# Attention and soft mixture of experts on one core: another written order, copies on the other engine, masks as steps of their own

## The chip, the core and the metric

The kernel runs on one core of one Trainium2 chip. The core has five instruction streams that run side by side and wait for each other by semaphores: TensorE (PE in the profile), VectorE (DVE), ScalarE (ACT), GpSimd (POOL) and SyncE (SP), which here only issues DMA transfers. Each stream runs in its own program order, so an instruction that waits holds back everything behind it in its stream. The metric is the time of one execution on the device, in microseconds (us).

## The reference

Attention over q, k and v of shape 8 x 8 heads x 576 x 64, with a mask by blocks of 64 (a block sees itself and earlier ones), then a soft mixture of 8 experts with 4 slots each on the result.

```python
scores = scale * np.matmul(q, k.transpose(0, 1, 3, 2))
mask = block_i >= block_j                      # blocks of 64 positions
attn = softmax(np.where(mask, scores, -1e9))
x = (attn @ v), heads side by side             # 4608 x 512
logits = x @ phi                               # 4608 x 32 slots
d = softmax of logits over tokens;  slot_input = d.T @ x
slot_out[e] = np.maximum(slot_input[e] @ w1[e], 0.0) @ w2[e]
c = softmax of logits over slots;   out = c @ slot_out
```

All of it is computed in float32.

## The kernel before, in words

The attention works through 32 pairs of heads, four pairs to one of the 8 batch entries. Pair m goes through these steps; the short names are the keys of the table `TM`:

- `lq`, `lk`, `lv` (SP, L403 to L418): DMA loads of q, k (288 KB each) and v (256 KB and a tail of 32 KB). q and k have two buffers and v has two, so the load for pair m+2 waits until PE is through with pair m.
- `ks` (POOL, L424): scales k in place. It waits for the landing of k.
- `UA`, `UB`, `UC` (PE, L464 and L485): the score tiles. The two 512 wide ones (`7`) come from UA, those of 576, 256, 192, 128 and 64 columns (`8`, `3`, `2`, `1`, `0`) from UB, and the two of 384 columns (`5`) from UC.
- `rm` (DVE, L507): row maximum of each tile. Ahead of the first `rm7` and of `rm5` the same function fills the masked 64 x 64 corners with a large negative number (L502, L505).
- `ex` (ACT, L517): exponential with the sum of each row. `ze` (POOL, L527) and `z` (DVE, L523): the inverses of the sums. `nm` (POOL, L534): the tile times its inverse, in place.
- `g7`, `gc`, `gd`, `g5` (PE, L554): transposes of the tiles by 64 x 64 blocks. gc takes tile 8, gd takes 3, 2, 1 and 0. `eg` and `og` (ACT L390 or DVE L392) copy them from PSUM to SBUF.
- `pv0`, `pv1`, `pa` (PE, L592 and L602): probabilities times v. `xb`, `xa`: copies of the result.

Between these stand the steps of the mixture for each batch entry: logits (`prt`), running maxima (`stats`), transposes of x (`xq`, `xn4`), and the weighted sums over tokens (`sl`, `sl4`). The weights of the experts come as 32 pieces of 1 MB each (L311): 18 go to places that nothing else uses, spread over the attention, and the others to places that the attention gives free. After pair 31 (from about 306 us on) the experts and the output follow.

The order is written out by hand: `TM` gives each step a time, steps are sorted by it, and each engine executes its steps in that order. The numbers of TM set nothing but the order. `EN` says for each copy whether ACT or DVE makes it, `BK` in which PSUM bank a step writes. Pairs 0 to 3 and the last two have their own entries (suffixes A to D, w and y); the others share four sets by m modulo 4 (suffixes .0 to .3). At L845 to L860 the steps get their times; L908 to L934 worked out from the times of the last readers when a weight piece may go to a place of the attention.

Of the kernel before, what the change touches and what calls it, by code (L numbers as in the profile page):

```python
# [21 lines left out]
NQ = 5  # L22
# [23 lines left out]
for name, n in (  # L46
# [18 lines left out]
    "T": 9.2, "lkA": -5.94771, "lqA": -2.81305, "lkB": -10.95031, "lqB": -8.91013, "ksA": -4.780053, "UAA":  # L65
# [3 lines left out]
    "ksB": -9.311415, "ze0A": 0.484236, "z0A": 4.153612, "ksC": 6.81181, "lkD": 5.110368, "rm8A": 4.053924, "lvA":  # L69
# [161 lines left out]
def tile_attention_softmoe(  # L231
# [99 lines left out]
    with ExitStack() as c1:  # L331
# [64 lines left out]
        def at(t, fn, *args):  # L396
            ops.append((t, len(ops), fn, args))
# [93 lines left out]
        def rowmax(m, x):  # L491
# [7 lines left out]
            if EN.get("Q" + x[0]) == "h":  # L499
                if x == "5":  # L500
                    for _, n, sc in todo:
                        nc.vector.memset(sc[0:64, :, 320:384] if n == 2 else sc[0:64, 320:384], NEG)  # L502
# [662 lines left out]
```

## Time and profile before

| what | us |
|---|---|
| median of 3 runs | 358.9 |
| the runs | 357.26, 358.90, 358.92 |
| span of the profiled execution | 357.1 |
| PE busy in that span | 342.2 (96%) |
| ACT, DVE, POOL busy | 272.0, 261.5, 205.0 |

The time of the profiled execution itself is not among the three runs. A run's time holds its span and a little around it; the lowest of the runs is 0.2 us above the span. PE's granted clock is full in all slices but the last. In the profile, an engine's idle time is given with what ended it; ends of matmuls are modelled, so that a short wait of PE can be hidden in a busy stretch.

### The profile page before, as it was taken

How to read it: one execution, taken by the hardware profiler on the slowest of the kernel's cores; microseconds unless marked ns; L12 is line 12 of the kernel's file. 1: busy time of each engine (PE TensorE's matmuls, PEld its weight loads, DVE VectorE, ACT ScalarE, POOL GpSimd, SP SyncE). 2: the span in 40 equal slices, each digit the busy share in tenths (PEclk: the TensorE clock that was granted, in tenths of full speed). 3: DMA queues.
4: the chain of work that ended last, by engine and by line, in shares of the span. 5: the costliest groups of instructions: out<-in, count | busy, mean ns of one | idle time of the engine just before them, and what ended most of it. 6: DMA issues, size and time to landing. Idle time of an engine off the chain costs nothing.

```text
span 357.1 us, 14425 instructions
## 1 busy us (share of the span) xinstructions
PE 342.2 (96%) x5724; PEld 237.1 (66%) x5724; DVE 261.5 (73%) x748; ACT 272.0 (76%) x869; POOL 205.0 (57%) x471
## 2 busy tenths in 40 slices
PE   8999999999999999999999999999999999999991
PEld 3767776677666766776767676776677677436750
DVE  4977777868887888777877887788888777462552
ACT  3988989888988898889888988899888875121441
POOL 3886767666766676567656766676687582000000
PEclk9999999999999999999999999999999999999996
DMA  6566526563664365743843556428333189999897
GB/s 198 182 211 229 163 74 212 199 225 101 184 224 133 102 218 186 249 106 114 292 135 101 204 195 211 148 70 312 127 104 102 36 253 331 375 397 397 327 373 298
DMA packets 29938, 72.29 MB, mean 202 GB/s; under 512 B 6960, under 2 KB 15280, under 8 KB 25520
## 3 DMA queue, kind: packets, MB, share of 16 engines
q1 hardware_dynamic: 29872, 71.38, 57.8%
q8 instruction: 45, 0.74, 0.8%
q14 instruction: 21, 0.17, 0.1%
HBM read 61.93 MB, written 9.44 MB: 200 GB/s over the span
## 4 chain that ended last, share of the span: by engine, by line
PE 79%; DVE 10%; POOL 5%; issue 3%; ACT 1%; DVEq 0%; POOLq 0%
PE one L592 15%; PE one L554 14%; PE one L464 7%; PE duo L464 7%; PE one L602 6%; PE one L485 5%; DVE stat L507 5%; POOL arena L534 4%; PE one L1088 4%; PE one L326 4%; PE duo L485 3%; PE one L1041 2%; PE one L623 2%; PE one L792 2%; DVE arena L392 1%
## 5 line engine op out<-in xcount | busy, mean ns | idle before, releaser
L534 POOL TENSOR_SCALAR arena<-arena,stat 128x512 f32<-128x512 f32 (+6 forms) x288 | 152.2, 544 | 30.8 <-DVE one L505 13.2
L517 ACT ACTIVATE arena<-one,stat 128x512 f32<-128x512 f32 (+5 forms) x194 | 93.9, 501 | 8.4 <-DVE stat L507 7.0
L390 ACT COPY arena<-one 128x384 f32<-128x384 f32 (+2 forms) x170 | 79.2, 503 | 26.8 <-PE one L554 21.3
L554 PEld LDWEIGHTS one<-ident,arena 64*128 64x128 f32 x1600 | 65.6, 138 | 33.4 <-ACT arena L390 9.0
L554 PE MATMUL one<-ident,arena 64*128 64x64 f32 x1600 | 76.3, 228 | 3.5 <-DVE arena L392 2.1
L507 DVE TENSOR_REDUCE stat<-one 128x1 f32<-128x512 f32 (+5 forms) x194 | 78.3, 436 | 1.7 <-PE one L485 0.6
L592 PE MATMUL one<-arena 128*64 128x256 f32 (+2 forms) x640 | 76.1, 384 | 0.0
L392 DVE COPY arena<-one 128x384 f32<-128x384 f32 (+3 forms) x106 | 56.4, 541 | 23.6 <-PE one L592 17.6
L517 ACT ACTIVATE arena<-duo,stat 128x384 f32<-128x384 f32 (+1 forms) x94 | 59.6, 640 | 7.0 <-DVE stat L523 5.6
L507 DVE TENSOR_REDUCE stat<-duo 128x1 f32<-128x576 f32 (+1 forms) x63 | 53.9, 855 | 13.3 <-PE duo L485 7.9
L592 PEld LDWEIGHTS one<-arena 128*64 128x64 f32 x640 | 41.1, 137 | 29.8 <-issue 18.2
L527 POOL TENSOR_SCALAR stat<-stat 128x2 f32<-128x2 f32 (+1 forms) x96 | 18.7, 195 | 55.0 <-ACT arena L517 50.9
L485 PE MATMUL one<-arena 64*64 64x256 f32 (+3 forms) x512 | 42.0, 303 | 0.0
L517 ACT ACTIVATION_READ_ACCUMULATOR arena<-one,stat 128x1 f32 x194 | 41.3, 213 | 0.0
L485 PE MATMUL duo<-arena 64*64 64x288 f32 x256 | 38.3, 417 | 0.0
L464 PE MATMUL one<-arena 64*128 64x512 f32 (+1 forms) x132 | 38.1, 636 | 0.0
L485 PEld LDWEIGHTS one<-arena 64*64 64x64 f32 x512 | 35.7, 133 | 2.2 <-ACT arena L517 0.4
L464 PE MATMUL duo<-arena 64*128 64x384 f32 x124 | 28.0, 529 | 0.4 <-ACT arena L517 0.4
L602 PE MATMUL one<-arena 128*64 128x64 f32 x620 | 24.9, 227 | 0.4 <-ACT arena L390 0.4
L602 PEld LDWEIGHTS one<-arena 128*64 128x64 f32 x620 | 20.6, 137 | 5.9 <-ACT xn L390 2.7
L424 POOL TENSOR_SCALAR arena<-arena 128x576 f32<-128x576 f32 x32 | 21.5, 672 | 3.6 <-DMA arena<-in_k 3.0
L523 DVE RECIPROCAL stat<-stat 128x2 f32<-128x2 f32 (+1 forms) x96 | 15.8, 165 | 7.2 <-POOL stat L527 6.9
(157 smaller groups left out, 382.8 us busy)
## 6 DMA issues: line engine op xcount, KB each, us to landing
arena<-in_w SPq DMA_DIRECT2D x31, 1024.0 KB, 7.2
arena<-in_k SPq DMA_DIRECT2D x32, 288.0 KB, 3.1
arena<-in_q SPq DMA_DIRECT2D x32, 288.0 KB, 3.2
arena<-in_v SPq DMA_DIRECT2D x32, 256.0 KB, 3.5
out<-arena SPq DMA_DIRECT2D x12, 512.0 KB, 4.5
out<-arena SPq DMA_DIRECT2D x2, 1024.0 KB, 5.6
arena<-in_v SPq DMA_DIRECT2D x32, 32.0 KB, 3.4
xarea<-in_w SPq DMA_DIRECT2D x1, 1024.0 KB, 8.0
```

Of the source, the lines that this page charges most:

```text
L390: nc.scalar.copy(out=out, in_=in_)
L392: nc.vector.tensor_copy(out=out, in_=in_)
L424: nc.gpsimd.tensor_scalar(out=area(f"ks{m % NQB}"), in0=area(f"ks{m % NQB}"), scalar1=SCALE, scalar2=0.0, op0=ALU.mult, op1=ALU.add)
L464: nc.tensor.matmul(scores(t + str(j), m)[o, a:e], lhsT=q[r, lo + o.start:lo + o.stop], rhs=k[r, a:e], start=True, stop=True)
L485: nc.tensor.matmul(o, lhsT=a, rhs=b, start=True, stop=True)
L507: nc.vector.tensor_reduce(out=st[:, 0, u:u + n], in_=sc, axis=AX.XY if x == "8" else AX.X, op=ALU.max, negate=True)
L517: nc.scalar.activation(out=pr, in_=sc, func=AF.Exp, bias=st[:, 0, u:u + 1], accum_out=st[:, 1, u:u + 1],)
L527: nc.gpsimd.tensor_scalar(out=st[:, 2, c], in0=st[:, 1, c], scalar1=EPS, scalar2=1.0, op0=ALU.add, op1=ALU.mult)
L534: nc.gpsimd.tensor_scalar(out=pr, in0=pr, scalar1=st[:, 2, u:u + 1], scalar2=0.0, op0=ALU.mult, op1=ALU.add)
L554: nc.tensor.transpose(out=trbank(m, g)[i][:, 64 * n:64 * n + 64], in_=prob(m, x)[r, 128 * c:128 * c + 128], identity=ident[r, r],)
L592: nc.tensor.matmul(xps[m, 0][64 * j:64 * j + 64, lo:hi], lhsT=vs(m)[:, j, c, :], rhs=rhs, start=a, stop=z, skip_group_check=True,)
L602: nc.tensor.matmul(xps[m, 1][64 * j:64 * j + 64, 0:64], lhsT=vs(m)[:, j, c, :], rhs=arena[:, lo:lo + 64], start=(c == 0), stop=(c == NQ - 1),)
```

## The change

The table TM is new: nearly every step has another number, and the order of the engines follows from it. `EN` puts 12 copies of the four steady sets and of the mixture on the other engine, six each way, and a number of those of the first and the last pairs. `BK` gives some steps another PSUM bank. The fill of the masked corners is no longer a part of `rowmax`: it is a step `mask` with two times of its own per pair (`mk7`, `mk5`). The weight pieces that go to places of the attention have times of their own (`pc0` to `pc6`) in place of computed ones. The diff cut to its code, with one line of the tables:

```diff
 TM = {
-    "T": 9.2, "lkA": -5.94771, "lqA": -2.81305, "lkB": -10.95031, "lqB": -8.91013, "ksA": -4.780053, "UAA":
+    "T": 9.2, "lkA": -63.498943, "lqA": -54.803813, "lkB": -52.245575, "lqB": -51.593279, "ksA": -50.318905, "UAA":
...
@@ rowmax
-            if EN.get("Q" + x[0]) == "h":
-                if x == "5":
-                    for _, n, sc in todo:
-                        nc.vector.memset(sc[0:64, :, 320:384] if n == 2 else sc[0:64, 320:384], NEG)
-                elif (tm(m, "rm" + x), x) == min((tm(m, f"rm7{j}"), f"7{j}") for j in range(2)):
-                    for j in range(2):
-                        nc.vector.memset(scores(f"7{j}", m)[0:64, 448:512], NEG)
             for u, n, sc in todo:
                 nc.vector.tensor_reduce(
...
+        def mask(m, x):
+            i, n = bank("S" + x, sfx(m)), NC[x]
+            if i in WIDE:
+                nc.vector.memset(duo[i].rearrange("p (j c) -> p j c", j=2)[0:64, :, n - 64:n], NEG)
+            else:
+                for t in two(i):
+                    nc.vector.memset(t[0:64, n - 64:n], NEG)
...
+            for x in "75":
+                at(t0 + tm(m, f"mk{x}"), mask, m, x)
...
-        places = []
-        for o in range(0, W0, PIECE):
-            places.append((max(ends[k] for k, (lo, hi) in AREAS.items() if lo < o + PIECE and hi > o), o))
...
-        for t, dst in places:
-            at(t, load_piece, nxt, dst)
-            nxt += 1
+        places = [arena[:, o:o + PIECE] for o in range(0, W0, PIECE)] + [xarea[:, 0:PIECE]]
+        for i, dst in enumerate(places):
+            at(tb + TM[f"pc{i}z"], load_piece, RES + i, dst)
+        nxt = RES + len(places)
```

Three places of the order follow. Line numbers of the changed kernel are higher by 5 or 6 here: L534 and L540 are `nm`, L527 and L533 `ze`, L424 and L429 `ks`, L407 and L412 `lk`, L414 and L419 with L418 and L423 `lv`, L311 and L316 the weight pieces.

**Place 1, the first pairs.** On POOL before, at the end of pair 1 (stat_119 belongs to odd pairs, stat_118 to even ones):

```order
L534 TENSOR_SCALAR arena<-arena,stat_119 128x128
L527 TENSOR_SCALAR stat_118<-stat_118 128x2
L534 TENSOR_SCALAR arena<-arena,stat_119 128x192
L534 TENSOR_SCALAR arena<-arena,stat_119 128x256
L370 MEMSET c_all 128x1152
L424 TENSOR_SCALAR arena<-arena 128x576
L534 TENSOR_SCALAR arena<-arena,stat_118 128x512 x2
```

The same stretch of POOL in the changed kernel:

```order
L533 TENSOR_SCALAR stat_118<-stat_118 128x2
L540 TENSOR_SCALAR arena<-arena,stat_119 128x192
L540 TENSOR_SCALAR arena<-arena,stat_119 128x384
L429 TENSOR_SCALAR arena<-arena 128x576
L540 TENSOR_SCALAR arena<-arena,stat_119 128x256
L540 TENSOR_SCALAR arena<-arena,stat_118 128x512 x2
L375 MEMSET c_all 128x1152
```

The scaling of k for pair 3 now stands ahead of `nm3` of pair 1 (256 columns), which the transposes gd of pair 1 need; before it stood behind it. On SP before, from the first v load on:

```order
L414 DMA arena<-in_v 128x2x256
L418 DMA arena<-in_v 64x2x64
L414 DMA arena<-in_v 128x2x256
L418 DMA arena<-in_v 64x2x64
L407 DMA arena<-in_k 128x576
L906 DMA phi<-in_phi 128x128
L403 DMA arena<-in_q 128x576
L311 DMA arena<-in_w 128x2048
L403 DMA arena<-in_q 128x576
L407 DMA arena<-in_k 128x576
```

The same stretch of SP in the changed kernel:

```order
L419 DMA arena<-in_v 128x2x256
L423 DMA arena<-in_v 64x2x64
L412 DMA arena<-in_k 128x576
L419 DMA arena<-in_v 128x2x256
L423 DMA arena<-in_v 64x2x64
L914 DMA phi<-in_phi 128x128
L408 DMA arena<-in_q 128x576
L316 DMA arena<-in_w 128x2048
L408 DMA arena<-in_q 128x576
L412 DMA arena<-in_k 128x576
```

One of the two v loads (that of pair 0) has moved behind the k load of pair 2, and so behind the wait of that load; the last row of each is the k of pair 3.

**Place 2, pair 24, as in every fourth pair.** On POOL before, from the `ze` of the five middle tiles of pair 24 on:

```order
L527 TENSOR_SCALAR stat_118<-stat_118 128x5
L534 TENSOR_SCALAR arena<-arena,stat_118 128x256
L527 TENSOR_SCALAR stat_118<-stat_118 128x2
L534 TENSOR_SCALAR arena<-arena,stat_118 128x192
L534 TENSOR_SCALAR arena<-arena,stat_118 128x576
L527 TENSOR_SCALAR stat_119<-stat_119 128x2
L534 TENSOR_SCALAR arena<-arena,stat_118 128x384
L534 TENSOR_SCALAR arena<-arena,stat_118 128x128
L534 TENSOR_SCALAR arena<-arena,stat_118 128x64
L424 TENSOR_SCALAR arena<-arena 128x576
```

The same in the changed kernel:

```order
L533 TENSOR_SCALAR stat_118<-stat_118 128x5
L540 TENSOR_SCALAR arena<-arena,stat_118 128x512
L429 TENSOR_SCALAR arena<-arena 128x576
L540 TENSOR_SCALAR arena<-arena,stat_118 128x256
L540 TENSOR_SCALAR arena<-arena,stat_118 128x576
L533 TENSOR_SCALAR stat_118<-stat_118 128x2
L540 TENSOR_SCALAR arena<-arena,stat_118 128x128
L540 TENSOR_SCALAR arena<-arena,stat_118 128x192
```

The scaling of k for pair 26 has moved from behind the nine `nm` of pair 24 to a place ahead of seven of them, among them `nm8` (576 columns), which the transposes gc need. On SP before, from the v of pair 23 on (the last two are k and q of pair 26):

```order
L414 DMA arena<-in_v 128x2x256
L418 DMA arena<-in_v 64x2x64
L311 DMA arena<-in_w 128x2048
L414 DMA arena<-in_v 128x2x256
L418 DMA arena<-in_v 64x2x64
L407 DMA arena<-in_k 128x576
L403 DMA arena<-in_q 128x576
```

The same in the changed kernel:

```order
L419 DMA arena<-in_v 128x2x256
L423 DMA arena<-in_v 64x2x64
L408 DMA arena<-in_q 128x576
L419 DMA arena<-in_v 128x2x256
L423 DMA arena<-in_v 64x2x64
L316 DMA arena<-in_w 128x2048
L412 DMA arena<-in_k 128x576
L408 DMA arena<-in_q 128x576
```

A weight piece of 1 MB now stands directly ahead of this k load. It does so for pairs 10, 18 and 26.

**Place 3, the last pairs.** On SP before, from the k of pair 31 on (the two v loads are those of pairs 30 and 31):

```order
L407 DMA arena<-in_k 128x576
L403 DMA arena<-in_q 128x576
L414 DMA arena<-in_v 128x2x256
L418 DMA arena<-in_v 64x2x64
L414 DMA arena<-in_v 128x2x256
L418 DMA arena<-in_v 64x2x64
L311 DMA arena<-in_w 128x2048 x6
```

The same in the changed kernel, where the v of pair 31 comes first and that of pair 30 second:

```order
L408 DMA arena<-in_q 128x576
L412 DMA arena<-in_k 128x576
L316 DMA arena<-in_w 128x2048
L419 DMA arena<-in_v 128x2x256
L423 DMA arena<-in_v 64x2x64
L419 DMA arena<-in_v 128x2x256
L423 DMA arena<-in_v 64x2x64
L316 DMA arena<-in_w 128x2048 x5
```

The v of pair 30 has moved behind a weight piece and behind the v of pair 31, which waits until PE is through with pair 29.

## Rows read from the trace of the kernel before

**Rows 1.** Windows by stage: from:to, length, busy us (instructions), clock, DMA share, GB/s.

```profile
0.00:27.35 27.35, 25.80 (x306) 16.07 (x308) 19.30 (x69) 20.16 (x66) 18.58 (x48) 1.00 0.62 200
94.29:277.92 183.63, 181.86 (x3060) 129.81 (x3063) 147.23 (x428) 158.36 (x509) 125.99 (x286) 1.00 0.51 168
277.92:305.86 27.94, 27.06 (x481) 19.39 (x480) 22.27 (x63) 20.44 (x73) 14.38 (x34) 1.00 0.66 231
305.86:357.10 51.24, 41.89 (x792) 24.00 (x791) 21.62 (x44) 14.54 (x32) 0.00 (x0) 0.95 0.90 359
```

**Rows 2.** Waits of PE: who waited for whom, us in total, times, longest.

```profile
PE one L554 <- DVE arena L392: 2.1, 6, 0.4
...
PE one L554 <- POOL arena L534: 0.7, 2, 0.4
```

**Rows 3.** Timeline of PE, pair 1: start, duration, what, idle time before.

```profile
22.33 0.52 PE L554 MATMUL one<-ident,arena 64*128 64x64 f32 x10
23.24 0.96 PE L554 MATMUL one<-ident,arena 64*128 64x64 f32 x24 [0.39 <-POOL arena L534]
24.15 0.92 PE L464 MATMUL duo<-arena 64*128 64x384 f32 x4
```

**Rows 4.** Timeline of POOL in the same stretch.

```profile
22.71 0.48 POOL L534 TENSOR_SCALAR arena<-arena,stat 128x256 f32<-128x256 f32 x1
```

**Rows 5.** Line L407, the k load of pair 3: duration, start; time to landing.

```profile
L407 SPq DMA_DIRECT2D arena<-in_k x1: 406/406/406, 17.3 to 17.3; - x1
...
DMA to landing us min/median/max: 6.0/6.0/6.0
```

**Rows 6.** Windows: the transfers of the first pairs.

```profile
12.00:16.00 4.00, 3.95 (x73) 3.01 (x68) 3.87 (x12) 3.86 (x13) 3.74 (x10) 1.00 0.94 267
```

**Rows 7.** Timeline of POOL, pair 24.

```profile
226.22 0.20 POOL L527 TENSOR_SCALAR stat<-stat 128x5 f32<-128x5 f32 x1
227.80 0.48 POOL L534 TENSOR_SCALAR arena<-arena,stat 128x256 f32<-128x256 f32 x1 [1.37 <-DVE one L505]
...
229.63 0.75 POOL L534 TENSOR_SCALAR arena<-arena,stat 128x576 f32<-128x576 f32 x1
...
231.93 0.67 POOL L424 TENSOR_SCALAR arena<-arena 128x576 f32<-128x576 f32 x1
```

**Rows 8.** Line L407, the k load of pair 26.

```profile
L407 SPq DMA_DIRECT2D arena<-in_k x1: 334/334/334, 226.4 to 226.4; - x1
...
DMA to landing us min/median/max: 2.9/2.9/2.9
```

**Rows 9.** Timeline of SP: a weight piece ahead of a k load.

```profile
240.87 0.59 SPq L311 DMA_DIRECT2D arena<-in_w  x1
```

**Rows 10.** Line L407, that k load.

```profile
L407 SPq DMA_DIRECT2D arena<-in_k x1: 387/387/387, 244.8 to 244.8; - x1
...
DMA to landing us min/median/max: 4.2/4.2/4.2
```

**Rows 11.** Timeline of PE, gc of pair 24.

```profile
231.49 0.53 PE L554 MATMUL one<-ident,arena 64*128 64x64 f32 x10
```

**Rows 12.** Timeline of DVE, pair 23: maximum of tile 8, copy of egc.

```profile
213.53 0.75 DVE L507 TENSOR_REDUCE stat<-duo 128x1 f32<-128x576 f32 x1
214.19 0.48 DVE L392 COPY arena<-one 128x320 f32<-128x320 f32 x1
```

**Rows 13.** Timeline of SP, the last v loads.

```profile
276.26 0.57 SPq L414 DMA_DIRECT2D arena<-in_v  x1
...
285.73 0.55 SPq L414 DMA_DIRECT2D arena<-in_v  x1
286.38 0.56 SPq L418 DMA_DIRECT2D arena<-in_v  x1
```

**Rows 14.** Line L414, all v loads.

```profile
DMA to landing us min/median/max: 2.8/3.5/5.7
```

**Rows 15.** Timeline of PE, pa of pair 30.

```profile
290.62 0.80 PE L602 MATMUL one<-arena 128*64 128x64 f32 x20
```

More of the change, by code (lines that the diff above doesn't have):

```diff
@@ L64 @@
 TM = {
[L65 removed]
[3 rows of a table removed]
[L69 removed]
[14 rows of a table removed]
[L84 removed]
[9 rows of a table removed]
[L94 removed]
[11 rows of a table removed]
[L106 removed]
[43 rows of a table removed]
[L150 removed]
[20 rows of a table removed]
[L171 to L173 removed]
[8 rows of a table removed]
[L182 removed]
+    "T": 9.2, "lkA": -63.498943, "lqA": -54.803813, "lkB": -52.245575, "lqB": -51.593279, "ksA": -50.318905, "UAA":
[18 rows of a table added]
+    "eg7B": 17.42806, "gcB": 17.629994, "egcB": 18.89372, "ogcB": 20.640618, "gdB": 24.871992, "rm1C": 11.503796,
[9 rows of a table added]
+    "egcC": 24.080879, "ogcC": 23.907996, "gdC": 26.092617, "paC": 26.211311, "ex8D": 15.279941, "UCD": 17.671586,
[55 rows of a table added]
+    58.742458, "elgv": 59.858483, "xn4v": 60.437309, "ksw": 3.90571, "UAw": 5.596911, "en4av": 64.109341, "statsv":
[20 rows of a table added]
+    82.152535, "xay": 85.143121, "ogdy": 85.167927, "ndtv": 121.967082, "dispv": 129.784782, "comb0z": 12.925111,
+    "comb1z": 298.921493, "pv0y": 99.165986, "pv1y": 100.902646, "sl4v": 131.53894, "sacc4v": 144.826504, "xby":
+    134.736218, "slv": 206.773606, "saccv": 233.496169, "prt3z": 165.939248, "prt4z": 163.185429, "elgz": 178.68655,
[8 rows of a table added]
+    201.100636, "en3bz": 199.414267, "slBz": 208.044624, "saccBz": 208.430689, "siTBz": 211.504285, "siCBz":
[5 rows of a table added]
 }
 EN = {
[17 rows of a table removed]
[17 rows of a table added]
 }
 BK = {
[1 row of a table removed]
[1 row of a table added]
     0, "S7.1": 1, "SB.1": 1, "S8.1": 2, "S5.1": 2, "Tg7.1": 3, "Tg5.1": 3, "Tgc.1": 3, "Tgd.1": 3, "PB.1": 0,
@@ L208 @@
     "PB.3": 0, "PA.3": 0, "S7A": 0, "SBA": 3, "S8A": 2, "S5A": 0, "Tg7A": 3, "Tg5A": 0, "TgcA": 0, "TgdA": 3, "PBA":
[1 row of a table removed]
[L210 removed]
[1 row of a table added]
+    "PAB": 6, "S7C": 1, "SBC": 1, "S8C": 2, "S5C": 2, "Tg7C": 3, "Tg5C": 0, "TgcC": 0, "TgdC": 3, "PBC": 1, "PAC":
     1, "S7D": 1, "SBD": 1, "S8D": 2, "S5D": 2, "Tg7D": 3, "Tg5D": 3, "TgcD": 3, "TgdD": 3, "PBD": 0, "PAD": 0,
[5 rows of a table removed]
[5 rows of a table added]
 }
@@ L906, in tile_attention_softmoe @@
         at(2 * T + tm(2, "lq") - 0.01, lambda: nc.sync.dma_start(out=phi_sb, in_=phi))
-        def end(m, keys):
-            return m * T + max(tm(m, k) for k in keys) + 0.01
-        ends = {}
-        for k in AREAS:
-            m = NM - 2 if k in ("q0", "ks0", "v0", "p7_0_0", "p7_1_0", "p1_0") else NM - 1
-            pvs = ("pa", "pv0", "pv1")
-            ends[k] = end(m, ("UA", "UB", "UC") if k[0] in "qk" else pvs if k[0] == "v" or k[:2] == "pt" else GROUPS)
-        for i in XIN:
-            m = max(m for m in range(NM) if m % NXT == i)
-            b = m // NP
-            z = endz(b)
-            ends[f"x{i}"] = 4 * b * T + 0.01 + max(TM[x + z] for x in (miscz if z == "z" else misc) if x[:2] in ("pr", "xq", "xn"))
-        ends["phi"] = tb + max(TM[f"prt{i}z"] for i in (*range(NQ), "4B")) + 0.01
-        places = []
-        for o in range(0, W0, PIECE):
-            places.append((max(ends[k] for k, (lo, hi) in AREAS.items() if lo < o + PIECE and hi > o), o))
-        last_v = end(NM - 1, ("lq", "lk", "lv"))
-        places = [(max(t, last_v + 0.001 * i), arena[:, o:o + PIECE]) for i, (t, o) in enumerate(places)]
-        last_x = tb + 0.01 + max(TM[k] for k in TM if k[-1] == "z" and k[:2] in ("pr", "xq", "xn"))
-        places.append((max(last_x, places[-1][0] + 0.001), xarea[:, 0:PIECE]))
-        nxt = RES
-        for t, dst in places:
-            at(t, load_piece, nxt, dst)
-            nxt += 1
+        places = [arena[:, o:o + PIECE] for o in range(0, W0, PIECE)] + [xarea[:, 0:PIECE]]
+        for i, dst in enumerate(places):
+            at(tb + TM[f"pc{i}z"], load_piece, RES + i, dst)
+        nxt = RES + len(places)
         for i in range(2):
```

9 lines of the change are left out of this document (removed), and 271 rows, old and new, of tables (BK, EN, TM).

## The prediction, made before the changed kernel ran

> **What bounds the kernel now.** I read the windows by stage first [rows 1]. In the five batch entries from 94 to 278 us PE is busy 181.86 of 183.63 us at full granted clock, while ACT has 158.36, DVE 147.23 and POOL 125.99 in the same stretch. The reader is to see that PE bounds this stage, that all its visible idle time there is 1.8 us, and that a better order of the other engines has little to win. In the first 27 us PE idles 1.6 us, from 278 to 306 us 0.9 us. What follows 306 us, experts and output, idles PE most, but the diff leaves its code as it is.
>
> Next the list of waits [rows 2]: PE's largest single item is 2.1 us, six times 0.35 us, in which the transposes gd wait for a copy on DVE; then 0.7 us, twice, waiting for POOL's normalization. One of the two is the 0.39 us ahead of gd in pair 1 [rows 3]. PE's ends are modelled, so short waits can hide in its busy time. I take the visible 1.8 us as what order can win, and put a hidden part into the range alone.
>
> Then the order itself. PE's order in the steady pairs is nearly the same before and after: the same steps in the same sequence, a few neighbours swapped (g5 ahead of UC in every fourth pair, `sl4` ahead of `prt3`). So PE's own work is the same and the change can only make waits of PE shorter or longer. The question is which of the inputs of PE come later.
>
> **The change part by part.**
>
> *Masks.* The memsets are the same in number and kind, on the same engine, and stand again just ahead of their maxima or one or two short steps earlier. They cannot go ahead of the scores that they overwrite. I cost them at nothing; DVE hides them with 36 us of idle time in the five entries (183.63 less 147.23) [rows 1]. Without that cover one would cost its own length, and no more.
>
> *Copies on the other engine.* Twelve in the steady sets, six each way, so neither engine's sum moves by more than the differences between them. Zero, with the loss of any one copy late by its length as the bound, inside the range.
>
> *The 0.35 us wait of gd.* It ends with the copy egc on DVE, 214.19 to 214.67 us, which starts when the maximum of tile 8 has gone through (from 213.53 us) [rows 12]. That maximum needs the scores of UB, and in the new order it still stands directly ahead of this copy. One copy ahead of both has gone to ACT, but another has taken its place, and the end of UB holds the maximum in any case. I take no gain; the bound is the whole 2.1 us.
>
> *First pairs.* On POOL the scaling of k for pair 3 now stands ahead of `nm3` of pair 1, and gd of pair 1 needs that. POOL executes in order, so `nm3` waits for a transfer. The k of pair 3 is issued at 17.3 us and takes 6.0 us [rows 5]: it lands at 23.3 us. Behind it come the scaling, 0.67 us (the same form in [rows 7]), and `nm3`, 0.48 us [rows 4], so gd can start at 24.45 us at the earliest. Before, `nm3` was over at 23.19 us and gd began at 23.24 us [rows 3, 4]. In the new PE order g5 stands ahead of gd and fills part of the wait: the two together take 0.96 us [rows 3], half of it is still to do behind the wait, so UC of pair 2 starts at 24.45 + 0.48 = 24.9 us instead of 24.15, 0.8 us later. On SP the v of pair 0 has moved from the quiet first microseconds into this queue, ahead of the same k: 288 KB more at 267 GB/s [rows 6] are 1.1 us. If all of it falls on that k, the loss is 1.9 us. The other end is a k that lands before `nm3` would be due: then the 0.39 us go. I take 1.4 us, nearer the upper middle, because both moves point one way. Queued behind the waiting scaling on POOL are `nm3`, the two `nm7` of pair 2 and a memset; PE's gd, and everything behind it, waits for the first.
>
> By the Trainium skill (DMA: Bandwidth & Descriptors, section "Anatomy of one DMA — SWDGE (gpsimd) path") a transfer takes about 2.0 us plus its bytes at 436 GB/s, 2.7 us for 288 KB as an estimate. The trace agrees where the queue is empty (2.9 us [rows 8]) and not in this stretch (6.0 us). By that rule this term would be a gain of 0.4 us.
>
> *Every fourth pair, as pair 24.* On POOL the scaling of k for pair 26 stands ahead of seven `nm` of pair 24. Before, POOL sat idle 1.37 us behind `ze` at 226.42 us and went on with `nm3` at 227.80 us [rows 7]. Now it waits for the k that is issued at 226.4 us and lands 2.9 us later, at 229.3 us [rows 8]. Then scaling 0.67, `nm3` 0.48 and `nm8` 0.75 us [rows 7] end at 231.2 us. gc needs `nm8` at 231.49 us [rows 11]: no loss, with 0.3 us to spare, where before `nm8` ended at 230.38 us, with 1.1 us to spare. In three of these pairs (8, 16 and 24) SP now issues a weight piece directly ahead of that k. In three places before, a k load follows a weight piece by about 4 us, as it would here; the middle one of the three (piece at 240.87, k at 244.8 us) took 4.2 us [rows 9, 10]. With 4.2 us `nm8` ends at 232.5 us, and gc starts 1.0 us late. Zero and 1.0 us are the ends for each of the three; there the q load stood between, which here comes behind, so I take 0.6, together 1.8 us. PE has no idle time in these pairs that would take it up, since the later wait of 0.35 us hangs on UB itself and shifts with it.
>
> *Last pairs.* The v of pair 30 was issued at 276.26 us. Now it stands behind the v of pair 31, which waits for PE until 285.73 us and needs two issues of 0.55 and 0.56 us [rows 13]: 286.9 us. With the median of 3.5 us it lands at 290.4 us, with the longest (5.7) at 292.6 us [rows 14], its tail half a microsecond later. pa of pair 30 started at 290.62 us [rows 15]. A weight piece goes ahead of both v loads. Loss 0 to 2.0 us. Against it, gd and g5 stand better in this stretch, which can give back the other wait for POOL, 0.3 us (0.7 less 0.39 [rows 2, 3]). I take 0.3 us. Earlier weight pieces win nothing by this: PE's first use of them is behind 306 us.
>
> *The sum.* 1.4 + 1.8 + 0.3 = 3.5 us on the profiled execution, whose span is 357.1 us. Its own time is not given; the lowest run is 0.2 us above the span, so I put it at 357.3 us, and the changed kernel at 360.8 us for such an execution. The median of the runs is 1.6 us above that one; two of the three runs lie there. I predict midway between the two levels, 358.1 + 3.5 = 361.6 us.
>
> **The rivals.**
>
> *No change that can be told.* The waits on k do come, but PE's queue takes them up: hidden waits elsewhere in a cycle shrink as PE comes later. For it: PE, ACT and POOL follow each other closely, and the list of waits holds what was visible only. Against it: a wait of PE in a stage where it is busy 99% is paid back nowhere that the profile shows. By the skill's rule on transfers (named above) it would come out here too, since all k loads would land in time. Time: 358 to 360 us, 359.0 as its middle.
>
> *Faster.* One mechanism: the chain on DVE from `z` to the copy ahead of gd in every fourth pair. With a copy of 512 columns and the second maximum of tile 7 behind it, `z` of the middle tiles comes earlier, POOL's `nm` with it, and the copy ends in time, so the six waits of 0.35 us go, and that in pair 1 as well: 358.1 - 2.1 - 0.4 = 355.6 us; as far as the run shown at 357.26 us is the level, 354.8. It decides if the k loads land by 2.9 us in all pairs and the maximum of tile 8 is not held by UB. For it: PE's largest wait is just this one. Against it: the start of the maximum at the end of UB.
>
> **How the numbers follow.** About 0.5% of 358.9 us, 1.8 us, is what a measurement can tell from no change: below 357.1 is faster, above 360.7 slower. The forecast gets a chance of 0.50, no change 0.30, faster 0.20. Within the forecast the ends are 1.9 + 3.0 + 2.0 us above and 0.8 + 0 + 0 below, so about 359.0 to 364.5 us by itself; a tenth of it falls under the bound of slower, and a part of the second rival's upper end above it. Faster 0.20, same 0.30, slower 0.50. The range takes the forecast's upper end nearly whole and the rival without change, and leaves out most of the faster case: 357.0 to 364.2 us.
>
> **What would show each step.** In the changed profile: POOL's L429 waiting for the landing of k near 22 to 24 us, with PE idle ahead of the transposes of line L560, released by POOL's L540, for 1 to 2 us; the same at gc of pairs 8, 16 and 24, with k loads of 4 us behind a weight piece; pa of pair 30 waiting for a v load. The batch entries should keep 36.7 us (183.63 / 5), those three longer by half a microsecond or more. The forecast is wrong if POOL waits for no k load, if the six waits of gd are gone, or if the k of pair 3 lands before 22 us.

## The result, and the profile after

The changed kernel takes 362.65 us (median of six runs, 361.35 to 365.74) against 358.8 us (six runs, 357.26 to 359.94) for the kernel before: a ratio of 1.0119, 95% interval 1.0084 to 1.0154. The span of the profiled execution grows by 4.0 us, from 357.1 to 361.1.

The windows of the changed kernel, cut at the same steps of the program as [rows 1] (columns as there):

```profile
0.00:28.11 28.11, 25.57 (x306) 15.38 (x308) 20.17 (x71) 20.09 (x65) 18.11 (x47) 1.00 0.60 196
96.17:281.63 185.46, 183.27 (x3061) 130.26 (x3063) 145.36 (x423) 157.96 (x516) 126.27 (x285) 1.00 0.50 162
281.63:309.95 28.32, 27.23 (x482) 19.30 (x482) 20.47 (x63) 20.74 (x72) 13.95 (x36) 1.00 0.66 245
309.95:361.10 51.15, 41.45 (x788) 23.56 (x788) 22.77 (x46) 15.10 (x33) 1.16 (x1) 0.94 0.87 351
```

The five batch entries take 1.8 us more, at the same granted clock (1.00) and with no more work on DVE, ACT or POOL (POOL 0.3 us more, the other two less). The last stage is as long as before. The windows show only 0.4 us of the 1.8 as idle time of PE (1.77 us before, 2.19 now); the rest stands there as longer busy time of the same matmuls, since their ends are modelled and can hide a wait. That it is waiting is read from the starts below. The list of PE's waits, as [rows 2] (who waited for whom, us in total, times, longest):

```profile
PE one L560 <- POOL arena L540: 2.4, 7, 0.5
PE one L560 <- DVE arena L397: 1.2, 5, 0.2
...
PE one L608 <- DMA arena<-in_v: 0.5, 2, 0.3
```

The wait for POOL's normalizations has gone from 0.7 us, twice, to 2.4 us, seven times (gd of pair 1, gc of pairs 3, 8, 16 and 24, gd of pair 28, g5 of pair 30); the wait for DVE's copy from 2.1 to 1.2 us. And POOL itself now waits for k loads (its list, before 3.0 us, three times):

```profile
POOL arena L429 <- DMA arena<-in_k: 13.4, 7, 2.8
```

In pair 24 this looks as follows, on POOL (start, duration, what, idle time before; before in [rows 7]):

```profile
228.91 0.20 POOL L533 TENSOR_SCALAR stat<-stat 128x5 f32<-128x5 f32 x1 [1.20 <-ACT arena L523]
229.20 0.69 POOL L540 TENSOR_SCALAR arena<-arena,stat 128x512 f32<-128x512 f32 x1
232.66 0.67 POOL L429 TENSOR_SCALAR arena<-arena 128x576 f32<-128x576 f32 x1 [2.76 <-DMA arena<-in_k]
233.31 1.20 POOL L540 TENSOR_SCALAR arena<-arena,stat 128x256 f32<-128x256 f32 x2
```

The last row holds `nm3` and `nm8` together. gc of pair 24 starts when they are over (PE's timeline, [rows 11] before):

```profile
234.56 0.53 PE L560 MATMUL one<-ident,arena 64*128 64x64 f32 x10 [0.22 <-POOL arena L540]
```

The chain that ended last runs through that load; before, no k load of these pairs was in it. Here is the stretch of the chain (start, us, what), and that of pair 28, where the k of pair 30 is late:

```profile
229.11 3.40 DMA arena<-in_k
...
232.66 0.67 POOL arena L429
233.33 1.18 POOL arena L540 x2
...
234.56 0.53 PE one L560 x10
...
267.94 3.66 DMA arena<-in_k
```

To see where the 4.0 us arise I compare starts of the same PE step in both traces. The lag of a step is its start in the other trace less its start before.

| step | before | changed | lag |
|---|---|---|---|
| UB of pair 0 | 6.52 | 6.46 | -0.06 |
| UA of pair 5 | 43.03 | 44.29 | 1.26 |
| UA of pair 9, then 10 | 79.12, 88.61 | 80.28, 90.54 | 1.16, 1.93 |
| UC of pair 12, UA of pair 13 | 115.32, 116.02 | 117.19, 118.21 | 1.87, 2.19 |
| UA of pair 17, then 18 | 152.71, 162.20 | 154.90, 164.85 | 2.19, 2.65 |
| UA of pair 25, then 26 | 226.11, 235.59 | 228.85, 238.82 | 2.74, 3.23 |
| UA of pair 29, then 30 | 262.79, 272.28 | 266.03, 275.99 | 3.24, 3.71 |
| gd of pair 29 | 278.85 | 282.55 | 3.70 |
| end of the span | 357.1 | 361.1 | 4.0 |

So 1.3 us arise in the first pairs, 2.45 in the steady pairs and 0.3 behind them. Pairs 8, 16 and 24 add 0.77, 0.46 and 0.49 us, pair 28 adds 0.47, and UA of pair 13 0.32: 2.5 us, all of the steady pairs' loss to within 0.1 us.

### The profile page after: what moved, and what is told of

It is laid out like the page before. It is cut to its first block, busy times and chain, and to the rows that moved or that the text cites. A ratio compares the mean times of both kernels' runs of the same rounds, so it can differ in the third digit from the quotient of the medians.

```text
span 361.1 us, 14407 instructions
## 1 busy us (share of the span) xinstructions
PE 343.3 (95%) x5724; PEld 235.9 (65%) x5724; DVE 260.2 (72%) x750; ACT 270.8 (75%) x867; POOL 205.6 (57%) x471
## 4 chain that ended last, share of the span: by engine, by line
PE 77%; DMA 5%; DVE 5%; POOL 4%; ACT 4%; issue 2%; SPq 1%; DVEq 0%; POOLq 0%
PE one L598 17%; PE one L560 14%; PE one L469 8%; PE duo L469 6%; PE one L608 5%; PE one L490 5%; PE one L331 4%; PE one L1073 4%; POOL arena L540 3%; DMA arena<-in_k 3%; PE duo L490 3%; ACT arena L523 2%; PE one L1026 2%; DMA arena<-in_v 2%; PE one L798 2%
## 5 line engine op out<-in xcount | busy, mean ns | idle before, releaser
L540 POOL TENSOR_SCALAR arena<-arena,stat 128x512 f32<-128x512 f32 (+6 forms) x288 | 153.1, 544 | 48.9 <-DVE stat L529 40.9
L395 ACT COPY arena<-one 128x384 f32<-128x384 f32 (+3 forms) x152 | 72.5, 503 | 29.2 <-PE one L560 25.9
L560 PEld LDWEIGHTS one<-ident,arena 64*128 64x128 f32 x1588 | 62.8, 138 | 34.2 <-ACT arena L395 7.7
L397 DVE COPY arena<-one 128x384 f32<-128x384 f32 (+3 forms) x122 | 65.2, 546 | 21.6 <-PE one L598 12.1
L505 DVE TENSOR_REDUCE stat<-one 128x1 f32<-128x512 f32 (+4 forms) x194 | 78.2, 437 | 0.6 <-PE one L490 0.2
L598 PEld LDWEIGHTS one<-arena 128*64 128x64 f32 x640 | 41.4, 137 | 30.0 <-issue 18.1
L469 PE MATMUL one<-arena 64*128 64x512 f32 (+1 forms) x132 | 37.1, 634 | 0.1
L533 POOL TENSOR_SCALAR stat<-stat 128x2 f32<-128x2 f32 (+1 forms) x96 | 18.7, 195 | 28.8 <-ACT arena L523 22.7
L429 POOL TENSOR_SCALAR arena<-arena 128x576 f32<-128x576 f32 x32 | 21.5, 672 | 16.5 <-DMA arena<-in_k 13.4
L608 PE MATMUL one<-arena 128*64 128x64 f32 x640 | 25.9, 227 | 1.7 <-DVE arena L397 0.6
L608 PEld LDWEIGHTS one<-arena 128*64 128x64 f32 x640 | 21.4, 137 | 7.9 <-ACT xn L395 3.3
```

The source lines that it names most:

```text
L395: nc.scalar.copy(out=out, in_=in_)
L397: nc.vector.tensor_copy(out=out, in_=in_)
L429: nc.gpsimd.tensor_scalar(out=area(f"ks{m % NQB}"), in0=area(f"ks{m % NQB}"), scalar1=SCALE, scalar2=0.0, op0=ALU.mult, op1=ALU.add)
L469: nc.tensor.matmul(scores(t + str(j), m)[o, a:e], lhsT=q[r, lo + o.start:lo + o.stop], rhs=k[r, a:e], start=True, stop=True)
L505: nc.vector.tensor_reduce(out=st[:, 0, u:u + n], in_=sc, axis=AX.XY if x == "8" else AX.X, op=ALU.max, negate=True)
L533: nc.gpsimd.tensor_scalar(out=st[:, 2, c], in0=st[:, 1, c], scalar1=EPS, scalar2=1.0, op0=ALU.add, op1=ALU.mult)
```

## The experiments

Twelve kernels ran. Six start from the changed kernel and put parts of the order back, six start from the kernel before and put parts of the change in. Only numbers of the table TM are edited, so each diff gives those. The table has the ratio to the kernel before, and from one profiled execution of each the lag that arises in three stretches: from UB of pair 0 to UA of pair 5, on to gd of pair 29, and on to the end of the span. Counting from UB of pair 0 leaves out the first 6 us, which differ by up to 1.2 us between executions (last section). Each lag is that of one execution. How far to trust it can be read from b1 to b6, which change nothing in the first pairs and nothing behind gd of pair 29: their first pairs agree with the kernel before within 0.03 us, but their ends lie between -0.3 and 1.3 us, so the last column tells nothing.

| kernel | ratio (95%) | first pairs | steady | end |
|---|---|---|---|---|
| changed | 1.0119 (1.0084 to 1.0154) | 1.3 | 2.45 | 0.3 |
| a1: k scaled late | 1.0081 (1.0052 to 1.0109) | 1.3 | 1.0 | 0.9 |
| a2: k ahead of piece | 1.0079 (1.0048 to 1.0110) | 1.1 | 0.7 | 0.2 |
| a3: first pairs | 1.0105 (1.0062 to 1.0148) | 0.8 | 2.3 | 0.3 |
| a4: all undone | 1.0065 (1.0039 to 1.0092) | 0.8 | 1.1 | 0.4 |
| a5: q first too | 1.0088 (1.0057 to 1.0118) | 2.5 | 0.05 | 0.0 |
| a6: first copies too | 1.0077 (1.0047 to 1.0108) | 2.4 | 0.05 | 0.0 |
| b1: before, k scaled early | 1.0131 (1.0100 to 1.0162) | 0.0 | 3.4 | 1.3 |
| b2: and k ahead of a v | 1.0072 (1.0049 to 1.0096) | 0.0 | 2.2 | 0.2 |
| b3: before, q late | 1.0063 (1.0039 to 1.0086) | 0.0 | 2.1 | 0.5 |
| b4: b1, nm8 second | 1.0100 (1.0075 to 1.0124) | 0.0 | 4.7 | -0.3 |
| b5: b4, z2 behind | 1.0016 (0.9992 to 1.0039) | 0.0 | 0.7 | 0.3 |
| b6: b5, piece ahead of k | 1.0059 (1.0039 to 1.0080) | 0.0 | 2.05 | 0.2 |

The intervals of most of these ratios overlap; what tells the theories apart is the lag of the first and of the steady pairs, and the waits.

**a1, the scaling of k late.**

```diff
-    "ks.2": 1.859256, "ksw": 3.90571
+    "ks.2": 4.05, "ksw": 4.05
```

> The changed kernel, but in every fourth pair the scaling of k for pair m+2 stands on POOL behind all seven small maxima's normalizations of pair m, as before the change. My theory: it is the wait for the landing of k ahead of nm8 that makes gc of pairs 8, 16 and 24 late (0.8, 0.5 and 0.5 us in the changed profile) and gd of pair 28 (0.45 us). With the scaling behind them the span goes from 361.1 to about 358.9 us and POOL waits for no k in these pairs. Rival one: POOL would have waited for DVE's inverses at that place anyway, so the wait only changes its name; then the span stays above 360.3 us. Rival two: the late scaling makes UA of pair m+2 late; then PE idles ahead of UA there and the span is 360 us or more.

Measured: span 359.2 us. The waits at gc of pairs 8, 16 and 24 and at gd of pair 28 are gone, and POOL waits 2.7 us for k, twice, about as before the change (3.0 us, three times). The steady lag falls from 2.45 to 1.0 us, not to 0.2: a wait appears that the changed kernel did not have. PE's timeline at UA of pair 7:

```profile
61.99 1.13 PE L469 MATMUL one<-arena 64*128 64x512 f32 x4 [0.43 <-DMA arena<-in_q]
```

The q of that pair stands behind a weight piece and a v on SP, where before it stood ahead of the v. PE, earlier by what the k wait had cost, now meets it. The theory holds for the waits and misses this one behind them; rival two has the right place for the wrong reason (UA waits for q, not for the scaling).

**a2, k ahead of the weight piece.**

```diff
-    "lk.2": 0.214442
+    "lk.2": -0.02
```

> The changed kernel, but on SP the k of pairs 10, 18 and 26 goes ahead of the weight piece instead of directly behind it; the scaling stays early. My theory: the early scaling costs only where the k is slow behind the piece. These k loads land 2.7 to 2.9 us after their issue instead of 3.4 to 3.7, nm8 ends 0.6 to 0.8 us earlier, and the loss at gc of pairs 8, 16 and 24 (1.8 us together) falls to 0.2 us at most; pair 28 keeps its 0.45 us. Span about 359.5 us. Rival: the place of the scaling alone costs, whatever the load takes; then these pairs keep 0.4 us or more each and the span stays above 360.5 us.

Measured: span 358.1 us, steady lag 0.7 us. The k of pairs 10, 18 and 26 land 2.7 to 2.9 us after issue and gc of pairs 8, 16 and 24 waits no more; pair 28 still loses 0.3 us, while its k (that of pair 30) takes 3.5 us. Of PE's waits for POOL two are left, ahead of gc of pair 3 and of g5 of pair 30:

```profile
PE one L560 <- POOL arena L540: 0.9, 2, 0.5
```

In the changed order the early scaling costs only where the load is slow. The rival is out for this kernel.

**a3, the first pairs.**

```diff
-    "lvA": 14.933988, "z1D": 21.125876
+    "lvA": -41.0, "z1D": 19.2
```

> The changed kernel, but the v of pair 0 is issued ahead of the wait for k's buffer, in the first microseconds as before, and on DVE the inverses z of the middle tiles of pair 3 stand ahead of a copy and of the two maxima of tile 7 of pair 4. The scaling of k for pair 3 stays ahead of nm3 of pair 1. Theory from the changed profile: the loss of the first pairs is 0.4 us in pa of pair 0, which waits for the tail of v (landing at 16.3 us), and 0.4 us at gc of pair 3, which waits for nm8 behind those inverses; together 0.8 us go, span 360.3 us. Rival, the step of my prediction: the scaling of k ahead of nm3 of pair 1 is what costs in the first pairs; then the span stays within 0.3 us of 361.1, and UA of pair 4 stays 1.2 us later than before the change.

In this kernel and the next, the inverses of pair 3 stand ahead of the sums that they invert and take older ones, so the normalizations of pair 3 wait for POOL's own sums and not for DVE; a5 has both in their order, and gc of pair 3 does not wait there either. Measured: the lag of the first pairs falls from 1.3 to 0.8 us. The scaling ahead of `nm3` is still there, and the lag is the same at UA and at UC of pair 2, on both sides of gd of pair 1 (-0.33 and -0.30 us): it costs nothing here. The span, 359.8 us, is lower than expected because this execution was 0.6 us faster in its first 6 us. The step of the prediction is out.

**a4, all loads and scalings back.**

```diff
+    "ks.2": 4.05, "ksw": 4.05, "lvA": -41.0, "z1D": 19.2, "lq.1": 1.80, "lvw": 13.0, "ksD": 4.0
```

> The changed kernel with all its late loads and scalings put back: scaling of k late in every fourth pair and in pairs 1 and 28, v of pair 0 in the first microseconds, inverses z of pair 3 early, q of pair 13 ahead of the weight piece (it landed 7.3 us after its issue behind one, and UA of pair 13 came 0.3 us late), v of pair 30 ahead of the pieces and of the v of pair 31. Masks as steps of their own and all copies stay as changed. My theory: 2.2 + 0.8 + 0.3 us and some 0.3 us of the last pairs come back: span about 357.5 us, ratio to before 1.00 within 0.003. Rival: the masks, the copies on the other engine or the order of the other engines cost themselves; then the span stays at 358.5 us or more, with PE's waits on DVE or ACT longer than before.

Measured: span 359.5 us, so the expected 357.5 is missed. The first pairs are as in a3 although the scaling of k for pair 3 now stands late as well, so its place makes no difference. The steady pairs keep 1.1 us: again the late q, at UA of pairs 19 and 23, where the lag grows by 0.5 and 0.25 us. Whether the rest was the rival's was open.

**a5, q right behind k.**

```diff
+    (as a4 without "ksD", but) "ze1D": 19.265, "z1D": 19.29, "lq.3": -2.5
```

> The changed kernel with all of the last experiment put back, and besides the q of pairs 7, 11, 15 and so on right behind their k on SP, ahead of weight piece and v. (The inverses z of pair 3 stand as early as their sums allow.) My theory: with the k waits gone, the next that PE met was the late q: it idled 0.35 us ahead of UA of pair 19 and 0.1 ahead of that of pair 23. Both go. The lag behind the kernel before at UA of pair 31, less that at UA of pair 2, was 3.0 us in the changed profile and 1.6 us with all of the last experiment; now about 0.8 us, and the ratio to before falls under 1.006. Rival: the lag left in the steady pairs is that of the copies and of the order on DVE and ACT; then it stays at 1.4 us or more.

One entry of a4 is not in this kernel: the scaling of k for pair 3 (`ksD`) stays as early as in the change. Measured: no wait for q, and from UA of pair 5 to gd of pair 29 the lag grows by 0.05 us (1.82 to 1.87). The whole steady loss was the place of loads and of the scaling; masks as steps of their own, the copies and the order on DVE and ACT cost PE nothing there, all taken together. But this execution met another wait in pair 3:

```profile
43.70 0.80 PE L608 MATMUL one<-arena 128*64 128x64 f32 x20 [1.61 <-DMA arena<-in_v]
```

The v of pair 3 took 8.5 us where in a4, with the same loads in the same order in this stretch, it took 5.5. The ratio did not fall under 1.006 as expected; whether the runs that were not profiled met this wait too is not known. The theory is shown for the steady pairs alone.

**a6, two first copies ahead.**

```diff
-    "egcA": 16.428119, "ogcC": 23.907996
+    (as a5, and) "egcA": 15.85, "ogcC": 23.888
```

> As the last version of the changed kernel (all loads and scalings put back, q right behind k), and besides two copies of the first pairs moved ahead on DVE: egc of pair 0 ahead of the maxima of tiles 1 and 8 of pair 1, and ogc of pair 2 ahead of the maximum of tile 8 of pair 3. They end the waits of PE ahead of pa of pair 0 (0.58 us) and of pa of pair 2 (0.63 us), and each pa starts 0.3 us later against the kernel before than the step in front of it. Theory: these 0.6 us come back; from UB of pair 0 to UA of pair 4 the lag goes from 1.2 us to about 0.6 (0.5 of it is only UA and g7 changing places). Rival: the maxima behind the copies come 0.45 us later, the exponentials with them, and PE waits for a bank instead; then the lag stays at 1.0 us or more.

Measured: the rival. The waits for the two copies shrink and come back elsewhere, on PE:

```profile
15.51 0.80 PE L608 MATMUL one<-arena 128*64 128x64 f32 x18 [0.73 <-ACT arena L395]
...
34.30 0.92 PE L469 MATMUL duo<-arena 64*128 64x384 f32 x4 [0.76 <-ACT arena L523]
```

The maxima behind the copies come late, the exponentials with them, and the bank of UC is free 0.76 us late. The lag of the first pairs is 2.4 us.

**b1, the early scaling in the kernel before.**

```diff
-    "ks.2": 4.552338
+    "ks.2": 2.6
```

> The kernel before, with one edit: on POOL the scaling of k for pair m+2 stands ahead of all nm of the small tiles in every fourth pair, as the change puts it. SP is as before, so no weight piece goes directly ahead of these k loads. My theory: k lands 2.9 us after its issue, about 1.5 us later than POOL was ready for nm3; nm8 is then over about 0.3 us before gc needs it, and PE loses at most 0.2 us in each of six such pairs: span within 0.8 us of the kernel before. Rival: an early scaling costs by itself; then gc of all these pairs waits 0.4 us or more and the span grows by over 2 us.

Measured: 1.0131, no faster than the change itself, although no piece stands directly ahead of these k and they land 2.7 to 3.3 us after issue. gc of pairs 8, 12, 16, 20 and 24 starts 0.52, 0.37, 0.98, 0.47 and 0.53 us later against the kernel before, 2.9 us together; the most is lost in pair 16, whose k took the 3.3 us. Another 0.6 us of the steady lag arise at gd of pair 10, where POOL had waited for a k whose scaling is in its old place and which took 5.2 us in this execution (4.6 before). The expectation failed: its end of `nm8` was worked out with the changed kernel's order behind the scaling (`nm3`, `nm8`), while here a `ze` and `nm2` stand between.

**b2, k behind the piece and ahead of the v.**

```diff
-    "ks.2": 4.552338, "lk.2": 1.950674
+    "ks.2": 2.6, "lk.2": 0.2
```

> As the run with the early scaling in the kernel before, and besides the k of pairs 10, 18 and 26 directly behind the weight piece and ahead of the v. My theory: these three k land 3.4 to 3.7 us after issue, and gc of pairs 8, 16 and 24 loses 0.5 to 0.8 us each, as in the changed kernel: the span grows by 1.5 to 2.3 us against the run without the piece. Rival: the piece has done most of its bytes when k starts, so that it takes nothing: then both runs agree within 0.3 us in these pairs.

Measured: the piece takes nothing from the k, as the rival has it. The edit made the two neighbours in the queue and not in time: the piece was issued at 71.5 us and landed at 78.9, and the k waited for its buffer until 78.8. These k landed in 2.6 to 2.9 us, and the five gc lose 2.4 us, 0.5 less than in b1; the difference lies in pair 16, where the k now took 2.8 us in place of 3.3.

**b3, q late in the kernel before.**

```diff
-    "lq.3": -0.569666
+    "lq.3": 5.0
```

> The kernel before, with one edit: on SP the q of pairs 7, 11, 15 and so on stands behind the v of the pair before, as the change puts it. My theory: this is a second, hidden cost of the change. Without the k waits PE is early enough to meet it: UA of some of these pairs (7, 19, 23 above all) starts 0.1 to 0.5 us late, together 0.5 to 1.2 us. Rival: the queue has slack for it and PE does not wait for q at all, so the waits seen in the other experiments come from the scaling alone; then the span stays within 0.3 us of the kernel before in the steady pairs.

Measured: 2.1 us, more than expected, most of it in one place. PE at UA of pair 11:

```profile
99.10 1.13 PE L464 MATMUL one<-arena 64*128 64x512 f32 x4 [1.07 <-DMA arena<-in_q]
```

The same late q is in the change. Its cost shows up there only in part, since PE comes later for other reasons: the parts of a loss do not add up.

**b4, nm8 second.**

```diff
-    "ks.2": 4.552338, "nm8.0": 22.279841
+    "ks.2": 2.6, "nm8.0": 21.1
```

> The kernel before with the early scaling of k in every fourth pair, and besides nm8 of the same pair directly behind nm3 instead of behind a ze and nm2. My theory, corrected by the last runs: gc starts when k has landed plus everything that POOL does from the scaling to the end of nm8. That was 2.85 us with ze and nm2 in it and 2.05 us in the changed kernel's order. With nm8 second the wait of gc of pairs 8, 12, 16, 20 and 24, 2.9 us together with the early scaling alone, falls by about 0.7 us each and all but vanishes: 0.5 us at most is left, in pair 16 above all. Rival: what costs is that POOL as a whole comes late in these pairs; then gd or g5 of the same pairs waits instead and 1.5 us or more of the 2.9 stay.

Measured: worse, 4.8 us at the five gc instead of 2.9. `nm8` ends 1.2 us before gc starts, so gc waits for something else. PE's row of gc in pair 24, and DVE's rows there:

```profile
235.83 0.52 PE L554 MATMUL one<-ident,arena 64*128 64x64 f32 x10 [0.90 <-POOL stat L527]
```

```profile
234.93 0.17 DVE L523 RECIPROCAL stat<-stat 128x2 f32<-128x2 f32 x1 [2.13 <-POOL stat L527]
235.01 0.67 DVE L392 COPY arena<-one 128x512 f32<-128x512 f32 x1
```

The reciprocal is `z2`, the inverse for tile 5. It needs POOL's `ze`, which is behind the scaling, and it stands ahead of the copy eg7 on DVE. So POOL's wait for k becomes a wait of DVE, eg7 is late, and gc writes to the bank that eg7 reads. The row names POOL's `ze`, the last step of that chain with a wait of its own; that eg7 is the missing link is read from DVE's rows. In b1 the same reciprocal waits 1.31 us. In the changed kernel `z2` stands behind eg7 and egc, at 235.66 us in pair 24, and cannot hold them up.

**b5, z2 behind the copies** (and nm51 behind nm0 on POOL, so that POOL does not wait for z2).

```diff
-    "ks.2": 4.552338, "nm8.0": 22.279841, "z2.0": 21.509813, "nm51.0": 22.563628
+    "ks.2": 2.6, "nm8.0": 21.1, "z2.0": 23.045, "nm51.0": 23.05
```

> The kernel before with the early scaling and nm8 second, as in the last run, and besides on DVE the inverse z of tile 5 (z2) behind the copies eg7 and egc of the same pair instead of ahead of eg7, as the changed kernel has it (and nm51 behind nm0, so that POOL does not wait for it). My theory, corrected again: in the last two runs z2 waited for POOL's ze behind the scaling, 1.3 and 2.1 us, DVE stood, eg7 came late and its bank was not free for gc. With z2 behind the copies DVE no longer waits for POOL there. gc waits for nm8 alone, which ends 2.05 us after k has landed: the waits of gc in pairs 8, 12, 16, 20 and 24, 4.7 us together in the last run, fall to 0.3 us at most in all. Rival: late nm and z in these pairs hit gd or g5 instead; then 1.5 us or more stay.

Measured: 1.0016 (0.9992 to 1.0039). No gc of these pairs waits. POOL still waits for k as long as in b4 (first fence, pair 24), DVE no longer does (second), and gc starts at once (third):

```profile
229.31 0.68 POOL L424 TENSOR_SCALAR arena<-arena 128x576 f32<-128x576 f32 x1 [2.88 <-DMA arena<-in_k]
229.97 1.21 POOL L534 TENSOR_SCALAR arena<-arena,stat 128x256 f32<-128x256 f32 x2
```

```profile
230.30 0.69 DVE L392 COPY arena<-one 128x512 f32<-128x512 f32 x1 [0.85 <-PE one L554]
...
232.70 0.15 DVE L523 RECIPROCAL stat<-stat 128x2 f32<-128x2 f32 x1
```

```profile
231.51 0.52 PE L554 MATMUL one<-ident,arena 64*128 64x64 f32 x10
```

POOL waits 18.6 us for k in this kernel, eight times, and the time is that of the kernel before within the interval. The two edits were made together and not told apart.

**b6, and a piece directly ahead of k.**

```diff
+    (as b5, and) "lv.0": 18.3, "lk.2": 0.2
```

> As the run with z2 behind the copies, and besides a weight piece issued directly ahead of the k of pairs 10, 18 and 26, as in the changed kernel (the v that stood between goes ahead of the piece). My theory: these k land 3.4 to 3.7 us after issue instead of 2.8, so gc of pairs 8, 16 and 24 waits 0.3 to 0.6 us each and pairs 12 and 20 do not: 0.9 to 1.8 us more than without the piece, the steady part of the changed kernel's loss rebuilt inside the kernel before. Rival: the piece takes nothing from the k here; then both runs agree within 0.3 us in these pairs.

Measured: 1.0059. gc of pairs 8, 16 and 24 waits 0.91, 0.37 and 0.10 us longer, 1.4 us together, pairs 12 and 20 not at all. The k of pairs 10 and 26, each right behind its piece (issue, time to landing):

```profile
L407 SPq DMA_DIRECT2D arena<-in_k x1: 334/334/334, 78.7 to 78.7; - x1
...
DMA to landing us min/median/max: 4.0/4.0/4.0
...
L407 SPq DMA_DIRECT2D arena<-in_k x1: 334/334/334, 227.2 to 227.2; - x1
...
DMA to landing us min/median/max: 3.2/3.2/3.2
```

The one that takes 4.0 us loses most, the one of 3.2 us least. Within the kernel before, these edits alone rebuild the loss of pairs 8, 16 and 24: 1.4 us at gc as in the change, and 2.0 us from UA of the next pair to UA of the one behind it, where the change has 1.7. No version that ran is faster than the kernel before.

## Why the prediction came out, step by step

The time lies 1 us above the forecast, inside the range, and the likeliest case happened: slower, by about the sum of 3.5 us (4.0 measured). That the sum comes so close is in part luck: two of its terms have about the right size for a reason that the runs do not bear out. The range itself was not added up cleanly: by its own text the first pairs could also win 0.4 us, and it counted 0.8 as their lower end; its ends add up to 365.0 us where it says 364.5. The measured time lies inside either way.

*Bound by PE, masks nothing: right for the steady pairs.* In a5 the steady lag is 0.05 us with masks and copies as changed.

*Every fourth pair, 1.8 us: right, in mechanism and size.* Measured 0.77 + 0.46 + 0.49 = 1.7 us. The step took a k of 4.2 us and, for each pair, 0.6 of the 1.0 us that would follow; it was 3.7, 3.4 and 3.4 us, and gc starts as the step has it: landing at 232.51 us, then the scaling, `nm3` and `nm8`, 234.4 us, measured 234.56. In a3, with the same order in these pairs, they lose 0.61, 0.90 and 0.04 us: the sum holds, the share of each pair changes with the execution. By the Trainium skill (DMA: Bandwidth & Descriptors, section "Anatomy of one DMA — SWDGE (gpsimd) path") 288 KB take an estimated 2.7 us; the section measured transfers issued by GpSimd, and these are issued by SyncE. The 2.7 to 2.9 us of a2 agree with it, the 3.4 to 3.7 us of the changed kernel do not. What the step did not see is that its order on POOL was safe only because `z2` had been moved as well (b1, b4 against b5): the same early scaling in the kernel before costs 2.9 us at its five gc. "Queued behind" was asked of POOL and PE and not of DVE. And pair 28 with the k of pair 30 was missing in the count: 0.47 us more. No piece is on its way there; the q of pair 30 and the v of pair 28 are issued just ahead of that k.

*First pairs, 1.4 us: the size was right and the mechanism wrong.* The step said that the k of pair 3 lands at 23.3 us at least and holds up `nm3`. It landed at 21.8 us, 3.8 us after its issue, before POOL was ready for it. The 6.0 us of [rows 5] are the longest of all profiled executions: in the fourteen of this study the same load took 3.1 to 6.0 us. The bound was read from one execution as if it were the load's own time. In the six executions with the early scaling (changed, a1 to a3, a5 and a6) it landed at 21.8 us at the latest; what a k of 6.0 us would do behind this order was not seen. POOL in the changed kernel, pair 1:

```profile
22.13 0.99 POOL L540 TENSOR_SCALAR arena<-arena,stat 128x192 f32<-128x192 f32 x2
23.09 0.67 POOL L429 TENSOR_SCALAR arena<-arena 128x576 f32<-128x576 f32 x1
23.74 1.14 POOL L540 TENSOR_SCALAR arena<-arena,stat 128x256 f32<-128x256 f32 x2
```

Against [rows 4], the scaling stands ahead of `nm3` without waiting. This was named beforehand as a sign that the forecast is wrong ("lands before 22 us"), and for this step it is; that 1.4 us was forecast and 1.3 us arose is luck. The loss came from elsewhere. PE in pair 0, pair 1 (as [rows 3]):

```profile
15.46 0.69 PE L608 MATMUL one<-arena 128*64 128x64 f32 x16 [0.58 <-DVE arena L397]
16.33 0.34 PE L608 MATMUL one<-arena 128*64 128x64 f32 x4 [0.19 <-DMA arena<-in_v]
...
24.27 0.59 PE L560 MATMUL one<-ident,arena 64*128 64x64 f32 x12 [0.42 <-POOL arena L540]
```

pa of pair 0 starts 0.3 us late, behind the copy egc, which was ACT's before and which DVE now makes behind two maxima, and its last matmuls wait for the tail of the v of pair 0, which lands at 16.3 us. The prediction moved that v into the queue and asked only what it does to the k behind it, not who needs the v itself. In pair 3, gc waits for `nm8`, which comes late because z of that pair stands behind two maxima on DVE (0.4 us, gone in a3, a4 and a5). The wait ahead of gd of pair 1 is no loss: g5 stands ahead of it now. How much the copies of the first pairs cost is not settled: moving two of them ahead made it worse (a6).

*The six waits of 0.35 us: not as taken, and without effect.* They were taken as unchanged. They became five of 0.2 us, 1.2 us in all where 2.1 stood. PE won nothing by it: a5, whose steady lag is 0.05 us, has shorter waits of this kind too (1.5 us). Why they are shorter was not tested, and the faster rival, which had them gone and PE earlier for it, is not borne out.

*Last pairs, 0.3 us: the number, but only half of the step.* From gd of pair 29 on 0.3 us arise, and pa of pair 30 does wait for its v (second row). The gain that was to stand against it did not come: where PE waited 0.3 us for POOL before, it now waits 0.52 us, at g5 of pair 30 (first row).

```profile
291.92 0.59 PE L560 MATMUL one<-ident,arena 64*128 64x64 f32 x12 [0.52 <-POOL arena L540]
...
294.17 0.80 PE L608 MATMUL one<-arena 128*64 128x64 f32 x20 [0.34 <-DMA arena<-in_v]
```

In a4 that v has its old place, and 0.4 us still arise behind gd of pair 29. With the scatter of this stretch (-0.3 to 1.3 us in b1 to b6) the runs do not show what the step costs.

*What no term held:* the late q, 0.3 us in pair 13 (issued behind a piece, 7.3 us to its landing) and another 1.1 us that the k waits hid in this kernel (a4 against a5; 2.1 us in the kernel before, b3). The order of SP shows the q behind the v; the prediction read that stretch for k alone.

*The level.* The prediction put the profiled execution's own time 0.2 us above its span. In all runs with both numbers it is 1.7 to 2.1 us above: 357.1 us of span stand for 358.9 us, the median itself. With that, its own sum gives 362.4 us; measured 362.65.

## What to carry to other kernels

Price a step that waits for a load by everything queued behind it on its own engine, and then by what the other engines, each in its own order, have standing behind *their* wait for that engine: POOL's 2.9 us wait for k cost nothing, or about 1 us per pair, by the place of one 0.17 us reciprocal on DVE (b5, b4; one `nm` on POOL went along with it). When a load moves in a queue, ask both who needs that load and who needs the loads that now stand behind it. And when undoing a part gives back less than it took, look for the next wait that it had hidden: here the late q stood behind the late k.

## What the runs showed of the hardware that was not expected

The k loads of pairs 10, 18 and 26 (288 KB each) took 2.6 to 3.3 us in the seven executions where the last 1 MB piece had landed by their issue or did so within 0.7 us. In the other seven a piece issued 2.7 to 3.9 us earlier was still on its way, and they took 2.8 to 4.2 us, that of pair 26 five times 2.9 us or less. So a piece close ahead went with a slow load in most of these cases and not in all. The q of pair 13 behind a piece took 7.3 us, the k of pair 8, 2.4 us behind one, 5.5 us (both in the changed kernel).

The four matmuls of UA of pair 0 take 2.08 us in the execution before and 1.13 us in that of a1, with the granted clock at 1.00 in both:

```profile
4.51 2.08 PE L464 MATMUL one<-arena 64*128 64x512 f32 x4
```

```profile
4.33 1.13 PE L469 MATMUL one<-arena 64*128 64x512 f32 x4 [0.16 <-POOL arena L429]
```

Over the fourteen executions they take 1.13 to 2.08 us, and over the seven of the kernel before and of b1 to b6, whose steps are the same there, the same two ends. That is a difference of about 1 us which a comparison of two spans would have put down to the change; the two spans of the result escape it by luck (2.08 and 1.97 us). What sets it stays open.

Transfers issued in the same order take very different times from one execution to the next: the first weight piece 7.2 to 9.7 us in the eleven executions with the v of pair 0 among the first loads, and 6.2 to 6.4 us in the three where that v stands a little ahead of it; the k of pair 3 behind it 3.1 to 6.0 us in all fourteen. Why the piece is shorter there was not tested. The changed kernel's six runs spread over 4.4 us and the six of the kernel before beside them over 2.7 us, but seventeen later runs of the kernel before spread over 4.5 us, so the spread is no mark of the change.
